# Moving three per-batch transposes to TensorE, regrouping the adapter slots 2, 2, 1, 1, and splitting the last pair's values by score tile

## The chip, the cores and the metric

The kernel runs on one core of one Trainium2 chip. The metric is the device time of one launch in microseconds (us). Five runs of the kernel before gave 178.95, 179.54, 181.83, 183.27 and 183.28 us; their median is 181.83 us. The engines are called PE (TensorE), DVE (VectorE), ACT (ScalarE), POOL (GpSimd) and SP (SyncE, which here only issues transfers).

## The reference, cut to what matters

Four batches of eight heads, 768 positions, head size 64. Attention is masked by a hash: a query sees only the keys whose six sign bits agree with its own. The attention output, laid out as 3072 rows of 512, goes through a mixture of eight rank-16 adapters, two for each row.

```
q_bits = (q @ proj > 0);  k_bits = (k @ proj > 0)          # six bits each
scores = where(q_bucket == k_bucket, q @ k.T / 8, -1e9)
attn   = softmax(scores);  attn_out = attn @ v
x      = attn_out, transposed to (B*S, H*D)                # 3072 x 512
logits = x @ w_gate                                        # eight per row
two largest logits per row -> weights w
out    = x + sum over the two experts of w * (x @ A[e]) @ B[e]
```

## The kernel before, in words

The unit of work is a pair of heads: 16 pairs, four in each batch (`PPB` is 4). For a pair the score matrix is 2 heads x 6 key blocks x 768 queries, which is nine score tiles of 128 x 1024 in PSUM. `score(p, s)` (lines 306 to 315) issues two or three matmuls for tile s and one ACT exponential that writes it to SBUF in bf16. The hash is carried in the contraction: rows 64 to 69 of the operand tile `aug` are sign rows, so one matmul of 71 rows gives score and mask together. There are two score buffers (`ps_s`), so the matmuls of a tile wait until the exponential two tiles earlier is done.

The order of everything is written out by hand. `run` (line 554) walks over pairs p and over steps s = 0 to 8; each step issues a score tile and then some work for other pairs, chosen in `pair(p, s)` (line 599) and `moe_slot(p, s)` (line 532). Each engine takes its instructions in that order.

- `trans` (228) turns queries and keys by PE (`tr`) and copies them out of PSUM (`qkT`, line 244 on DVE, or 242 on ACT when `on_act`). Group 2 for pair p + 1 is at s = 0; groups 0 and 1 for pair p + 2 are at s = 4 and 5. Group 0 goes to ACT in pairs that have adapter work (`has_moe`, 528).
- `cast` (271, s = 1) puts them into `aug` on POOL. `hash` (251, s = 2) forms the signs (`hs` on PE, `sgn` on DVE, line 260) and issues two of the four sign transfers; `hash_b` (266, s = 5) issues the other two, for the pair's second head.
- `uniform` (s = 3) makes a constant (`un`, `uni`) that `norm` adds in line 365, except in the last four pairs, where PE adds it by a matmul (line 331).
- `pvmm` (319) multiplies attention by values: head 0 of pair p at s = 6, 7, 8, and head 1 of pair p - 1 at s = 1 and 3. Its accumulator `pv` is the single buffer of `ps_v`, so head 1 starts (line 320, s = 1) only after `norm(p - 1, 0)` at s = 0 has read it: lines 365 (add), 368 (reciprocal), 370 (product into `x`). `norm(p - 1, 1)` is at s = 4 and is followed by the bf16 copy `xb` on POOL (376).
- `xturn` (412, s = 5) turns `xb` of pair p - 1 into `xT` by a DMA transpose on SP. `xtrans` (420) does the same by PE, with up to six 128 x 128 transposes into a `ps_t` tile and a copy out by DVE (430); before, only the last pair and the one ahead of it use it.
- The adapters of a batch start in the second pair of the next batch (p = 5, 9, 13). A row slot is 128 rows; a batch has six. `lgz` (434, line 445, four matmuls of `lz` for each slot) needs `xT` of all four pairs of the batch. Then come `route_a`, `route_e`, `route_b` (454 to 490: `top`, `d`, `e` on ACT, `gw`, `zm`, `ss`, `rt`), `zmtrans` (498, 504), and `delta` (512 on PE; 519 on DVE adds to `x`), and a transfer out. Slots go in groups of two over three pairs for the first two batches, and in groups of three over two pairs for the third.

`ps_t` has two buffers and holds `tr`, `hs`, `un`, `xtp` (the PE-turned `xb`), in the last pair also one `pvl` and an `lz`. `ps_m` has one buffer, for `lz`, `ztp` and `dl`.

The last pair (`last_pair`, 634) orders its score tiles by thirds of the query blocks: tiles 0 to 2 belong to third 0, 3 to 5 to third 1, 6 to 8 to third 2. `third(u, part)` (380, line 398) multiplies a third by values in two parts; the second part ends with a reciprocal and a product on DVE (402, 408). After it come the adapters of the fourth batch, two slots for each third. Four of the six final additions are on POOL (517), each from a product that ACT makes (516).

Of the kernel before, what the change touches and what calls it, by code (L numbers as in the profile page):

```python
# [19 lines left out]
class Emitter:  # L20
# [355 lines left out]
            nc.gpsimd.tensor_copy(out=self.xb[b][:, hp], in_=self.x[b][:, :, hp * P:(hp + 1) * P])  # L376

    def third(self, u, part):  # L380
        nc, P, T, D = self.nc, self.P, self.T, self.D
        p, b = self.n_pairs - 1, self.B - 1
        if part == 0:
            pool, tag = (self.ps_t, "t") if u == 1 else (self.ps_v, "v")
            pv = pool.tile([P, 2, 2, D + 1], F32, tag=tag, name=f"pvl{u}")
            ri = self.smallp.tile([P, 2, 2], F32, tag="ri", name=f"ril{u}")
            self.pvl[u] = pv, ri
            nc.tensor.matmul(
                out=pv, lhsT=self.eps, start=True, stop=False,
                rhs=self.vb[p % 3][:, :, T, :].unsqueeze(2).to_broadcast([P, 2, 2, D + 1]))  # L390
        pv, ri = self.pvl[u]
        for h in range(2):
            kts = range(T) if h == 0 else range(2) if part == 0 else range(2, T)
            if h == 0 and part:
                continue
            for e in range(2):
                for kt in kts:
                    nc.tensor.matmul(out=pv[:, h, e, :], lhsT=self.p_at(p, h, kt, 3 * e + u),  # L398
                                     rhs=self.vb[p % 3][:, h, self.slot(kt), :], start=False,
                                     stop=(part == 1 and e == 1 and kt == T - 1))  # L400
        if part:
            nc.vector.reciprocal(out=ri, in_=pv[:, :, :, D])
            self.third_x(u, self.xb[b][:, self.PPB - 1])

# [120 lines left out]
            nc.sync.dma_start(out=rows[:, slots[0]:slots[0] + len(slots), :], in_=acc[:, 0:len(slots), :])  # L525


    def has_moe(self, p):
        b, g = divmod(p - self.PPB - 1, self.PPB)
        return 0 <= b < self.B - 1 and g < (3 if b < self.B - 2 else 2)  # L530

    def moe_slot(self, p, s):
        b, g = divmod(p - self.PPB - 1, self.PPB)
        if b < 0 or b > self.B - 2:
            return
        n = 2 if b < self.B - 2 else 3
        if n * g >= self.T:
            return
        slots = tuple(range(n * g, n * g + n))
        if s == 0:  # L540
            self.lgz(b, slots, (0,))
        if s == 1:
            self.lgz(b, slots, tuple(range(1, n)))
            self.route_a(b, slots, now=False)
        if s == 2:
            self.route_e(b, slots)
        if s == 3:
            self.route_b(b, slots)
        if s == 4:
            self.zmtrans(b, slots)  # L550
        if 0 <= s - 6 < n:
            self.delta(b, slots, s - 6)
# [46 lines left out]
    def pair(self, p, s):  # L599
        if s == 0:  # L600
            self.norm(p - 1, 0)
            self.trans(p + 1, 2)
            self.load_qk(p + 3, (0,))
        if s == 1:
            self.pvmm(p - 1, 1, 0, 3)
            self.cast(p + 1, 0)
            self.cast(p + 1, 1)
        if s == 2:
            self.hash(p + 1)
            self.load_qk(p + 3, (1,))  # L610
        if s == 3:
            self.uniform(p)
            self.pvmm(p - 1, 1, 3, 6)
        if s == 4:
            self.norm(p - 1, 1)
            self.trans(p + 2, 0, on_act=self.has_moe(p))
        if s == 5:
            self.xturn(p - 1)
            self.hash_b(p + 1)
            self.vcast(p + 1)  # L620
            self.trans(p + 2, 1)
            if p < 4:
                self.load_moe(p + 1)
            if p == 3:
                self.load_moe(5)
        if s == 6:
            self.pvmm(p, 0, 0, 2)
        if s == 7:
            self.pvmm(p, 0, 2, 4)
        if s == 8:  # L630
            self.pvmm(p, 0, 4, 6)
            self.load_v(p + 3)

    def last_pair(self, p, b):
        t = [(0, 1), (2, 3), (4, 5)]
        x = self.x[b][:, :, (self.PPB - 1) * self.P:]
        for s in range(9):
            self.score(p, s)
            if s == 0:
                self.norm(p - 1, 0)  # L640
                self.pvmm(p - 1, 1, 0, 3)
            if s == 1:
                self.pvmm(p - 1, 1, 3, 6)
                self.norm(p - 1, 1)
            if s == 3:
                self.third(0, 0)
            if s == 4:
                self.third(0, 1)
            if s == 5:
                self.xtrans(p - 1)  # L650
                self.xtrans(p, t[0])
                self.third_x(0, x)
            if s == 6:
                self.third(1, 0)
                self.lgz(b, t[0])
                self.route_a(b, t[0], now=False)
            if s == 7:
                self.route_e(b, t[0])
                self.third(1, 1)
                self.route_b(b, t[0])  # L660
            if s == 8:
                self.xtrans(p, t[1])
                self.zmtrans(b, t[0])
                self.third(2, 0)
                self.third_x(1, x)
        self.third(2, 1)
        self.lgz(b, t[1], far=True)
        self.route_a(b, t[1])
        self.delta(b, t[0], 0, last=True, by_pool=True)
        self.xtrans(p, t[2])  # L670
        self.route_b(b, t[1])
        self.delta(b, t[0], 1, last=True, by_pool=True)
        self.lgz(b, t[2])
        self.zmtrans(b, t[1], last=True, far=True)
        self.route_a(b, t[2])
        self.delta(b, t[1], 0, last=True, by_pool=True)
        self.third_x(2, x)
        self.route_b(b, t[2])
        self.zmtrans(b, t[2], last=True, far=True)
        self.delta(b, t[1], 1, last=True, by_pool=True)  # L680
        for i in range(2):
            self.delta(b, t[2], i, last=True)
# [47 lines left out]
```

## Time and profile before

| what | value |
|---|---|
| median of five runs | 181.83 us |
| the profiled execution's own time | 178.92 us |
| its span | 177.1 us |
| PE, ACT, POOL, DVE busy | 92%, 86%, 65%, 63% of the span |
| granted TensorE clock | 0.99 of full speed |
| 144 exponentials (line 315) | 140.3 us, 1030 ns each |
| 14 DMA transposes (line 416) | 1251 ns of SP each, in the median |

The profile is one execution, with times from the start of its span. The span is cut in 40 slices whose digits are busy tenths; PE shows 9 in nearly every slice from the second to the 37th. A matmul's record includes its way through the array, so matmuls overlap in the records: eighteen value matmuls are issued in 0.55 us, while their records cover 0.72 us. In the chain of waits the first of these figures is what counts.

### The profile page before, as it was taken

What the parts mean: (1) busy time and instruction counts of PE and PEld (TensorE: products, weight loads), DVE (VectorE), ACT (ScalarE), POOL (GpSimd) and SP (SyncE); (2) the same over time, 40 slices, a digit from 0 to 9 for tenths busy, and PEclk for the clock granted to TensorE, in tenths of its full rate; (3) what the DMA queues carried; (4) which work ended last, traced back from release to release, by engine and by line L of the source; (5) the groups of instructions that cost most, each with busy time, mean ns of one, the idle gap of its engine ahead of it and who ended that gap; (6) DMA issues with size and microseconds to landing.
All of it is one profiled execution on the core that took longest, in us unless ns stands there. A gap on an engine that the chain in (4) does not pass through costs nothing.

```text
span 177.1 us, 5185 instructions
## 1 busy us (share of the span) xinstructions
PE 162.1 (92%) x2073; PEld 111.8 (63%) x2074; DVE 111.7 (63%) x294; ACT 151.6 (86%) x174; POOL 115.5 (65%) x140
## 2 busy tenths in 40 slices
PE   7989999999996999999999999999999999989630
PEld 6356585857675666767577676667576774767500
DVE  4663574747474586869674786868554967536860
ACT  3678999999997998999999999999998998988440
POOL 8299998787976477565676476765677546710190
PEclk9999999999999999999999999999999999999995
DMA  5936599798998577697886488977884033540045
GB/s 163 329 135 184 160 262 102 214 122 223 108 251 105 177 125 239 188 152 261 146 257 147 142 133 295 129 208 228 170 262 122 4 97 137 52 183 4 0 157 198
DMA packets 32406, 29.10 MB, mean 164 GB/s; under 512 B 17430, under 2 KB 30590, under 8 KB 32382
## 3 DMA queue, kind: packets, MB, share of 16 engines
q1 hardware_dynamic: 27420, 28.50, 63.3%
q0 software_dynamic: 4832, 0.27, 4.7%
q8 instruction: 16, 0.26, 0.7%
q14 instruction: 8, 0.07, 0.1%
q10 hardware_dynamic: 130, 0.00, 0.0%
HBM read 19.42 MB, written 6.29 MB: 145 GB/s over the span
## 4 chain that ended last, share of the span: by engine, by line
PE 80%; DVE 5%; DMA 4%; ACT 3%; issue 2%; POOL 2%; POOLq 1%; SPq 0%
PE s L313 34%; PE pv L320 17%; PE tr L237 10%; PE hs L257 7%; ACT P L315 3%; PE lz L445 3%; PE dl L512 3%; DMA xT<-xb 2%; POOL acc L517 1%; DMA aug<-sgn 1%; PE warm L184 1%; PE pvl L398 1%; PE trf L125 1%; PE hsd L139 1%; POOLq L725 1%
## 5 line engine op out<-in xcount | busy, mean ns | idle before, releaser
L315 ACT ACTIVATE P<-s 128x1024 bf16<-128x1024 f32 x144 | 140.3, 1030 | 12.4 <-PE s L313 11.4
L313 PE MATMUL s<-aug 71*128 71x256 bf16 (+1 forms) x396 | 86.3, 320 | 2.9 <-issue 1.3
L275 POOL CAST aug<-qkT 64x1536 bf16<-64x1536 f32 x30 | 43.9, 1463 | 15.1 <-DVE qkT L244 14.2
L320 PEld LDWEIGHTS <-P 128*128 128x128 bf16 x1080 | 42.1, 97 | 11.5 <-DVE x L370 3.5
L313 PEld LDWEIGHTS <-aug 71*128 71x128 bf16 x396 | 33.1, 97 | 22.9 <-issue 11.6
L320 PE MATMUL pv<-vb,P 128*128 128x65 bf16 x1080 | 45.2, 193 | 0.2 <-DVE x L370 0.2
L376 POOL CAST xb<-x 128x768 bf16<-128x768 f32 x15 | 12.4, 824 | 26.2 <-DVE x L370 22.0
L237 PE MATMUL tr<-ident,nat 128*128 128x128 f32 x180 | 27.2, 272 | 0.0
L244 DVE TENSOR_SCALAR qkT<-tr 128x512 f32<-128x512 f32 x38 | 25.4, 683 | 2.7 <-PE tr L237 1.4
L237 PEld LDWEIGHTS tr<-ident,nat 128*128 128x128 f32 x180 | 21.8, 140 | 4.8 <-issue 0.6
L365 DVE TENSOR_TENSOR pv<-pv,uni 128x390 f32<-128x390 f32 x24 | 13.6, 567 | 10.9 <-PE pv L320 10.5
L519 DVE SCALAR_TENSOR_TENSOR acc<-dl,rt,x 128x512 f32<-128x512 f32 x20 | 14.9, 748 | 7.9 <-PE dl L512 7.9
L260 DVE TENSOR_SCALAR sgn<-hs 128x384 bf16<-128x384 f32 x15 | 8.4, 558 | 16.9 <-PE hs L257 16.9
L370 DVE TENSOR_TENSOR x<-pv,ri 128x384 f32<-128x384 f32 x30 | 16.7, 557 | 1.0
L221 POOL TENSOR_TENSOR vs<-vn 128x384 f32<-128x384 f32 x16 | 15.9, 994 | 0.0
L219 POOL CAST vb<-vn 128x768 bf16<-128x768 f32 x16 | 13.2, 827 | 0.1
L257 PE MATMUL hs<-qkT,proj 128*32 128x384 f32 x120 | 12.8, 498 | 0.0
L517 POOL TENSOR_TENSOR acc<-tmp,x 128x512 f32<-128x512 f32 x4 | 4.9, 1271 | 9.2 <-ACT tmp L516 9.2
L445 PE MATMUL lz<-wa,xT 128*128 128x136 bf16 x96 | 9.2, 223 | 1.2 <-DMA xT<-xb 1.2
L512 PE MATMUL dl<-Bcat,zmT 128*128 128x512 bf16 x23 | 8.8, 382 | 1.2 <-ACT zmT L502 0.7
L368 DVE RECIPROCAL ri<-pv 128x6 f32<-128x6 f32 x30 | 5.8, 193 | 3.9 <-PE pv L320 3.1
L224 POOL TENSOR_TENSOR vb<-vs,vs 128x128 bf16<-128x128 f32 x16 | 7.3, 459 | 1.3
(65 smaller groups left out, 111.8 us busy)
## 6 DMA issues: line engine op xcount, KB each, us to landing
vn<-in_v_dram SPq DMA_DIRECT2D x16, 384.0 KB
nat<-in_q_dram SPq DMA_DIRECT2D x15, 384.0 KB
nat<-in_k_dram SPq DMA_DIRECT2D x15, 384.0 KB
out_dram<-acc SPq DMA_DIRECT2D x6, 512.0 KB
out_dram<-acc SPq DMA_DIRECT2D x2, 768.0 KB
out_dram<-acc SPq DMA_DIRECT2D x6, 256.0 KB
aug<-sgn SPq DMA_DIRECT2D x60, 9.0 KB
nat<-in_q_dram SPq DMA_DIRECT2D x2, 192.0 KB
```

Source lines behind the costliest of these rows:

```text
L221: nc.gpsimd.tensor_add(out=s3, in0=vn[:, :, 0:3, :], in1=vn[:, :, 3:6, :])
L237: nc.tensor.transpose(out=ps[:, j * P:(j + 1) * P], in_=self.nat[p][:, idx % 2, idx // 2, u * P:(u + 1) * P], identity=self.ident)
L244: nc.vector.tensor_scalar(out=out, in0=ps, scalar1=2.0 ** -5, scalar2=None, op0=ALU.mult)
L257: nc.tensor.matmul(out=ps[32 * j:32 * j + 32, :], lhsT=self.proj2, rhs=self.qkT[p][:, j * 384:(j + 1) * 384], start=True, stop=True)
L275: self.nc.gpsimd.tensor_copy(out=self.aug[p % 2][0:64, :, e * n:(e + 1) * n], in_=self.qkT[p][64 * e:64 * e + 64, :].rearrange("p (j c) -> ...
L313: nc.tensor.matmul(out=ps[:, o:o + n], lhsT=aug[0:71, 2 * h + 1, kt * P:(kt + 1) * P], rhs=q, start=True, stop=True)
L315: nc.scalar.activation(out=self.P_[p][:, s * 1024:(s + 1) * 1024], in_=ps, func=ACT.Exp, scale=128.0)
L320: self.nc.tensor.matmul(out=pv, lhsT=self.p_at(p, h, kt, i), rhs=self.vb[p % 3][:, h, self.slot(kt), :], start=(start and kt == 0), stop=( ...
L370: nc.vector.tensor_tensor(out=self.x[b][:, :, c:c + D].rearrange("p (u e) d -> p e u d", e=2), in0=pv[:, 0:T, 0:D].rearrange("p (e u) d -> ...
L445: nc.tensor.matmul(out=lz[:, i, :], lhsT=self.xT[b][:, t, s * P:(s + 1) * P], rhs=self.wa[:, t, :], start=(t == 0), stop=(t == self.nD - 1))
L512: nc.tensor.matmul(out=ps, lhsT=self.zmT[b, slots][:, i * P:(i + 1) * P], rhs=self.Bcat, start=True, stop=True)
L519: nc.vector.scalar_tensor_tensor(out=acc[:, i, :], in0=ps, scalar=self.rt[b, slots][:, i:i + 1], in1=self.x[b][:, slots[i], :], op0=ALU.mu ...
```

## The change

Five edits, all in the written-out order:

1. At the first pair of the next batch (p = 4, 8, 12) the DMA transpose of a batch's last pair is dropped, and at the end of s = 8 `xtrans(p - 1)` turns it by PE, with the copy on DVE.
2. For the first two batches the groups of slots become (0, 1), (2, 3), (4), (5) over all four pairs. The third batch keeps 3 and 3. In a pair with a group of one slot, group 0 of `trans` is copied out by DVE, not by ACT.
3. For the last pair, the two sign transfers of its second head are issued in s = 2 of pair 14, not in s = 5 behind that pair's DMA transpose.
4. `third` has three parts, each of the four key blocks that one score tile holds; in steps 2 to 4, 5 to 7, and 8 and after.
5. In the last pair `xtrans(14)` goes from s = 5 to s = 4; behind the last score tile the order changes, and the first `zmtrans` goes behind the last third, its copy on ACT (line 502) in place of DVE.

```diff
@@ third(u, part)
-        for h in range(2):
-            kts = range(T) if h == 0 else range(2) if part == 0 else range(2, T)
-            if h == 0 and part:
-                continue
+        for j in range(4):
+            h, kt = divmod(4 * part + j, T)
             for e in range(2):
-                for kt in kts:
-                    nc.tensor.matmul(out=pv[:, h, e, :], lhsT=self.p_at(p, h, kt, 3 * e + u),
...
-        if part:
+        if part == 2:
@@ moe_group(p), in place of has_moe; moe_slot takes its slots from it
+        groups = ((0, 1), (2, 3), (4,), (5,)) if b < self.B - 2 else ((0, 1, 2), (3, 4, 5), (), ())
+        return b, groups[g]
@@ pair(p, s)
         if s == 2:
             self.hash(p + 1)
+            if p + 1 == self.n_pairs - 1:
+                self.hash_b(p + 1)
...
-            self.trans(p + 2, 0, on_act=self.has_moe(p))
+            self.trans(p + 2, 0, on_act=len(self.moe_group(p)[1]) > 1)
         if s == 5:
-            self.xturn(p - 1)
-            self.hash_b(p + 1)
+            if p % self.PPB:
+                self.xturn(p - 1)
+            if p + 1 < self.n_pairs - 1:
+                self.hash_b(p + 1)
...
         if s == 8:
             self.pvmm(p, 0, 4, 6)
+            if p % self.PPB == 0:
+                self.xtrans(p - 1)
@@ last_pair(p, b)
-            if s == 3:
-                self.third(0, 0)
+            if 2 <= s < 5:
+                self.third(0, s - 2)
             if s == 4:
-                self.third(0, 1)
+                self.xtrans(p - 1)
             if s == 5:
-                self.xtrans(p - 1)
                 self.xtrans(p, t[0])
                 self.third_x(0, x)
+            if 5 <= s < 8:
+                self.third(1, s - 5)
             if s == 6:
-                self.third(1, 0)
                 self.lgz(b, t[0])
                 self.route_a(b, t[0], now=False)
             if s == 7:
                 self.route_e(b, t[0])
-                self.third(1, 1)
                 self.route_b(b, t[0])
             if s == 8:
                 self.xtrans(p, t[1])
-                self.zmtrans(b, t[0])
+                self.third_x(1, x)
                 self.third(2, 0)
-                self.third_x(1, x)
         self.third(2, 1)
         self.lgz(b, t[1], far=True)
         self.route_a(b, t[1])
+        self.third(2, 2)
+        self.zmtrans(b, t[0], last=True)
+        self.xtrans(p, t[2])
         self.delta(b, t[0], 0, last=True, by_pool=True)
-        self.xtrans(p, t[2])
         self.route_b(b, t[1])
+        self.lgz(b, t[2])
         self.delta(b, t[0], 1, last=True, by_pool=True)
-        self.lgz(b, t[2])
         self.zmtrans(b, t[1], last=True, far=True)
```

More of the change, by code (lines that the diff above doesn't have):

```diff
@@ L391, in third @@
         pv, ri = self.pvl[u]
-        for h in range(2):
-            kts = range(T) if h == 0 else range(2) if part == 0 else range(2, T)
-            if h == 0 and part:
-                continue
+        for j in range(4):
+            h, kt = divmod(4 * part + j, T)
             for e in range(2):
-                for kt in kts:
-                    nc.tensor.matmul(out=pv[:, h, e, :], lhsT=self.p_at(p, h, kt, 3 * e + u),
-                                     rhs=self.vb[p % 3][:, h, self.slot(kt), :], start=False,
-                                     stop=(part == 1 and e == 1 and kt == T - 1))
-        if part:
+                nc.tensor.matmul(out=pv[:, h, e, :], lhsT=self.p_at(p, h, kt, 3 * e + u),
+                                 rhs=self.vb[p % 3][:, h, self.slot(kt), :], start=False,
+                                 stop=(part == 2 and j == 3 and e == 1))
+        if part == 2:
             nc.vector.reciprocal(out=ri, in_=pv[:, :, :, D])
@@ L525, in delta, with moe_group @@
             nc.sync.dma_start(out=rows[:, slots[0]:slots[0] + len(slots), :], in_=acc[:, 0:len(slots), :])
-    def has_moe(self, p):
+    def moe_group(self, p):
         b, g = divmod(p - self.PPB - 1, self.PPB)
-        return 0 <= b < self.B - 1 and g < (3 if b < self.B - 2 else 2)
+        if not 0 <= b < self.B - 1:
+            return b, ()
+        groups = ((0, 1), (2, 3), (4,), (5,)) if b < self.B - 2 else ((0, 1, 2), (3, 4, 5), (), ())
+        return b, groups[g]
     def moe_slot(self, p, s):
-        b, g = divmod(p - self.PPB - 1, self.PPB)
-        if b < 0 or b > self.B - 2:
+        b, slots = self.moe_group(p)
+        n = len(slots)
+        if not n:
             return
[L536 to L539, printed above, removed]
         if s == 0:
```

## The prediction

> **What bounds the kernel now.** I read the page's chain shares first, then busy time in single pairs, then the chain and the timelines around each edit.
>
> ```profile
> PE 80%; DVE 5%; DMA 4%; ACT 3%; issue 2%; POOL 2%; POOLq 1%; SPq 0%
> ```
>
> PE carries the chain. How hard it binds is seen by cutting single pairs out: no adapters (28.42 and 124.74), two slots (66.37 and 114.89), columns PE, PE weights, DVE, ACT, POOL.
>
> ```profile
> 28.42:37.34 8.92, 8.76 (x120) 6.15 (x118) 5.30 (x12) 8.57 (x10) 7.25 (x9) 1.00 0.92 166
> 66.37:76.21 9.84, 9.74 (x131) 6.82 (x130) 7.55 (x22) 9.37 (x12) 6.39 (x8) 1.00 0.85 198
> 114.89:124.74 9.85, 9.75 (x131) 6.83 (x130) 7.56 (x22) 9.38 (x12) 6.41 (x8) 1.00 0.79 199
> 124.74:133.70 8.96, 8.80 (x119) 6.08 (x118) 5.10 (x11) 8.63 (x10) 6.56 (x8) 1.00 0.75 224
> ```
>
> A pair lasts 8.92 to 8.96 us without adapters, 9.85 with two slots. PE is full in both, ACT half a microsecond behind. So PE work added to a pair counts unless a PE wait absorbs it.
>
> Two places are neither. The chain shows them:
>
> ```profile
> 51.64 0.83 POOL xb L376
> 52.49 4.42 DMA xT<-xb
> 57.63 0.55 PE pv L320 x18
> ...
> 153.52 2.31 DMA aug<-sgn
> 155.83 0.05 issue
> 155.88 0.41 PE s L313 x2
> 156.28 0.02 issue
> 156.31 1.03 ACT P L315
> ```
>
> Pair 5's first `lz` waits for the transpose issued at 52.49; the wait list has 1.4 us there for PE's weights, and ACT then idles 1.37. Pair 9 loses only about 0.1 (its four `lz` take 0.36 in the chain, those of pair 10 take 0.24), pair 13 nothing. Tile 1 of the last pair waits for signs issued at 153.5; ACT idles 0.75.
>
> **What the Trainium skill says.** "DMA: Bandwidth & Descriptors", section Anatomy of one DMA, puts most of a transfer's fixed cost, about 2 us, into the receipt at the end. The trace agrees for the signs (2.31 us); the transpose took 4.42. "PSUM — Partial Sum Buffer", section Engine vs sequencer instructions: the vector and scalar queues are strict FIFO and matmuls complete in program order. The trace agrees: DVE's `norm` stands behind whatever precedes it. "TensorE: Matmul & The Clock Gate", section PE-mode transpose: the result lands in PSUM and needs a DVE copy, about 275 ns in a kernel. Here a record is 221 ns, but six follow each other in 0.35 us of chain, so I use 0.33 of issue.
>
> **The change, part by part.**
>
> *PE transposes in pairs 4, 8, 12.* Each adds six transposes (0.33 us of PE) and one 128x768 copy (0.56 us, line 430) and removes one DMA transpose from SP (1.25 us; the sign transfers behind it go earlier, which nothing waits for there). In pair 4 PE stands still 0.16 us before pair 5's tile 0 and takes 0.59 for it instead of 0.44: 0.31 us of waiting for ACT covers the 0.33. Without that cover it would be 0.33 each time.
>
> The copy costs more than the transposes: DVE does it ahead of `norm(p - 1, 0)`, which frees the only `pv` buffer, and queued behind the waiting value matmuls on PE are tile 2, the hash and tile 3. In pair 9 now, value matmuls end issue at 94.16 and drain at 94.32; `norm` runs 94.36 to 95.75 and the next values start at 96.30. After: transposes 94.16 to 94.49, drained 0.2 later, copy 94.70 to 95.26, `norm` (starts 0.60, 0.23 apart, then 0.56) 95.30 to 96.70, values 96.76: +0.46. In pair 13 `norm` has no add (0.20 + 0.56): 134.76 against the present 134.65, +0.1. In pair 5 the same sum gives 54.25 + 2.60 = 56.86 against 57.46 now: the DMA wait goes but a wait for `norm` takes its place, −0.6 and not −1.3. `xT` itself is ready at 55.4, ahead of `lz` at 55.5.
> Sum: −0.6 + 0.46 + 0.1 = **0.0**.
>
> *Groups 2, 2, 1, 1 (pairs 7, 8, 11, 12).* PE work is the same over the batch: one slot is four `lz` at 0.059 = 0.24, `ztp` 0.055, `dl` 0.21: 0.5 us. ACT loses one `qkT` copy (0.59 record, 0.5 between neighbours), DVE gains one (0.60 from start to start). That one stands ahead of the `zmT` copy, for which `dl` waits, and behind `dl` stand the value matmuls and tile 7. Pair 11 on DVE now:
>
> ```profile
> 118.08 0.56 DVE L260 TENSOR_SCALAR sgn<-hs 128x384 bf16<-128x384 f32 x1 [0.79 <-PE hs L257]
> 118.65 0.29 DVE L352 COPY uni<-un 128x130 f32<-128x130 f32 x1
> 118.86 0.35 DVE L476 SCALAR_TENSOR_TENSOR gw<-lz,top,e 128x8 f32<-128x8 f32 x2
> 119.24 0.42 DVE L478 TENSOR_TENSOR zm<-lz,gw 128x256 bf16<-128x256 f32 x1
> ...
> 120.68 0.56 DVE L370 TENSOR_TENSOR x<-pv,ri 128x384 f32<-128x384 f32 x1
> 121.15 0.28 DVE L504 COPY zmT<-ztp 128x256 bf16<-128x256 bf16 x1
> ```
>
> DVE is in one piece from 118.08, and `dl` starts at 121.49, just as PE gets to it. With one slot, one `gw` (0.17) and half of `zm` (0.13) go, so the chain is 0.30 earlier; then `qkT` puts 0.60 in: `zmT` starts 121.45, ends 121.66, `dl` 121.72. PE gets there at 121.41: a new stall of 0.3 us. A pair with two slots that gets one: −0.5 + 0.3 = −0.2. A pair with none that gets one: +0.5 + 0.3 = +0.8, less about 0.2 that PE spends waiting for ACT at tiles 7 and 8 (0.50 and 0.55 in the chain where two matmul groups take 0.43) = +0.6. Together +0.4 a batch, two batches: **+0.8**. Bounds: −0.3 a batch, if the stall is covered and ACT's relief counts, to +0.8, if nothing is absorbed.
>
> *Signs in pair 14.* The two transfers (1.5 us of SP) come before any load, since there is none left; they can land near 153, tile 1 needs them at 155.4. ACT goes on at 155.5: **−0.75**.
>
> *Thirds, and the end.* Here most of the 0.75 is lost again. A third's last part still follows its last tile. The PSUM buffer of third 1 is the one `xtrans(14)` used: its copy ends about 1.3 us after third 0 and third 1 is now asked for 0.9 after, so PE waits 0.4 and ACT idles about 0.35 at tile 6; before, the same wait came one step later and cost 0.59 at tile 7. Tile 8's exponential ends near 163.8 instead of 164.62. Then `lz` of slots 2 and 3, whose PSUM buffer comes free with line 408's `x`, is moved ahead of the last part: now 165.56 to 165.58, after about 164.56. The last part queues behind it (0.47), and `top`, `d` (0.45 of DVE) stand ahead of its reciprocal: last `xb` 165.9 against 166.0. First `dl` stands behind the transposes of that `xb`, so ACT's first product is at 166.9 against 166.94. That starts what ends the kernel:
>
> ```profile
> 167.69 4.94 POOL L517 TENSOR_TENSOR acc<-tmp,x 128x512 f32<-128x512 f32 x4 [9.16 <-ACT tmp L516]
> ```
>
> Four additions back to back, then transfers. They start about 0.1 earlier. So edits 3 to 5 together give **−0.1**, between −0.75 (all kept) and +0.3 (new order later than the old).
>
> *Sum:* 0.0 + 0.8 − 0.1 = **+0.7 us** on the profiled execution's 178.92 (span 177.1 and 1.8 around it): 179.6. That execution is in the lower of two groups of runs (178.95, 179.54; 181.83 to 183.28). The mean of five is 181.37, the median 181.83. A median of five jumps between the groups, so I put the change on the mean: **182.1 us**.
>
> **The rivals.**
>
> A. *Both waits gone, little put in their place.* If PE's lead hides the `norm` wait and the 0.3 stalls: −1.2 (pair 5), −0.1, −0.75 kept, groups 0: −2.0, or 179.4. For it: ACT loses 1.0 us of copies over two batches and DVE is only 76% busy in adapter pairs. Against: pairs without a DMA wait already show a wait for line 370 of up to 0.6, ten times.
>
> B. *DVE becomes the bound, slower.* Place: `zmT` ahead of `dl` in pairs 7, 8, 11, 12. If the DVE queue is late there by 1.2 us and not 0.3, because ACT's late `e` holds `gw` too, each costs 0.9 more: 0.7 + 3.6 = +4.3, or 185.7. It decides from a stall of about 1.0 on (+3.5). Against: DVE has 2.3 us free in such a pair.
>
> C. *The upper runs are late transposes.* If in those runs pairs 9 and 13 also wait 1.3 for the DMA, taking it away puts them near the lower group: 181.4 − 2 × 1.3 = 178.8 to 179.6. For it: one landing took 4.42 us, others left no wait. Against: 0.1 seen in pair 9, and no trace of an upper run.
>
> **How the numbers follow.** My forecast 0.5, A 0.25, C 0.15, B 0.06, the rest for what I do not see. The forecast's own range is 179.6 to 184: the two groups plus 0.7. A and C lie at 178.8 to 179.6, so the low end is 178.2 (lowest run less 0.75, the signs alone); the high end 184.2 is the highest run plus 0.9. B is left out. About 2% is what a measurement of this kernel can tell from no change: 178.2 and 185.5. My forecast lies inside, A and C at their faster ends (0.08), B beyond the other end (0.06): same 0.86.
>
> **What would show it.** Right: no `xT` wait in pair 5, but 0.5 to 0.7 us of PE waiting for line 370 there and in pair 9; PE waiting near 0.3 for `zmT` in four pairs; pairs 7 and 8 at about 9.65 and 9.55; no sign wait at the last pair; POOL's four additions starting as long before the span's end as now (9.4 us). Wrong: pairs 8 and 12 under 9.2, or values of pair 9 no later after tile 0 than now, or a last stage shorter by over 0.5.

## The result, and the profile after

The ratio of the changed kernel to the kernel before is 1.0038 (95% interval 1.0022 to 1.0054): a slow-down of 0.4%, about 0.7 us, clear of the spread and far within 2%. The medians over all runs, 179.82 us (44 runs) and 179.96 us (79 runs), show it the other way round because 22 of the 79 runs of the kernel before lie above 181.21 us, the slowest of the changed kernel's, and the ratio leaves out runs as far up as these. The profiled execution took 179.35 us (before: 178.92), its span 177.6 us (177.1).

The page's chain shares after. PE's share has fallen from 80% to 68%, DVE's has risen from 5% to 13%; DMA, 4% before, is gone.

```profile
PE 68%; DVE 13%; POOL 7%; ACT 4%; issue 3%; POOLq 1%
```

The transfers that the chain held are out of it, and vector work has come in. To see where, both kernels are cut into pairs, from the first `tr` record of one pair to that of the next. Kernel before, pairs 5, 7, 8, 9, 11, 12 and 13 (columns: length, then busy time of PE, PE weights, DVE, ACT, POOL, then granted clock, DMA share, GB/s):

```profile
55.01:66.20 11.19, 9.92 (x131) 6.82 (x130) 7.45 (x22) 9.48 (x12) 6.24 (x8) 1.00 0.56 129
76.05:85.90 9.85, 9.75 (x132) 6.83 (x131) 7.56 (x22) 9.38 (x12) 6.41 (x8) 1.00 0.78 199
85.90:94.91 9.01, 8.85 (x120) 6.15 (x118) 5.40 (x12) 8.66 (x10) 6.55 (x8) 1.00 0.78 222
94.91:104.88 9.97, 9.87 (x132) 6.83 (x130) 7.46 (x22) 9.38 (x12) 6.25 (x8) 1.00 0.66 139
114.73:124.58 9.85, 9.75 (x132) 6.83 (x131) 7.56 (x22) 9.38 (x12) 6.41 (x8) 1.00 0.79 198
124.58:133.53 8.95, 8.79 (x119) 6.08 (x118) 5.06 (x12) 8.62 (x10) 6.55 (x8) 1.00 0.75 224
133.53:143.93 10.40, 10.36 (x139) 7.37 (x137) 6.45 (x20) 9.55 (x12) 6.67 (x8) 1.00 0.26 64
```

The changed kernel, the same pairs:

```profile
54.82:65.25 10.43, 9.92 (x131) 6.75 (x130) 8.24 (x23) 9.47 (x12) 6.22 (x8) 1.00 0.59 123
75.10:84.81 9.71, 8.99 (x125) 6.42 (x124) 6.97 (x20) 8.96 (x11) 6.76 (x8) 1.00 0.95 201
84.81:94.55 9.74, 9.16 (x130) 6.68 (x130) 6.58 (x20) 8.99 (x11) 6.41 (x8) 1.00 0.62 189
94.55:104.98 10.43, 9.92 (x132) 6.75 (x131) 8.25 (x23) 9.35 (x12) 5.99 (x8) 1.00 0.57 130
114.83:124.59 9.76, 8.99 (x125) 6.42 (x125) 7.00 (x20) 9.01 (x11) 6.80 (x8) 1.00 0.89 200
124.59:134.19 9.60, 9.28 (x130) 6.73 (x130) 6.26 (x18) 8.90 (x11) 6.39 (x7) 1.00 0.60 190
134.19:144.58 10.39, 10.35 (x138) 7.29 (x137) 7.10 (x22) 9.51 (x12) 6.39 (x7) 1.00 0.28 62
```

Pair 5 is 0.76 us shorter, pair 9 0.46 longer and now exactly as long as pair 5: both wait for the same thing. Pairs 8 and 12, which got a slot, grew by 0.73 and 0.65; pairs 7 and 11, which gave one away, shrank by 0.14 and 0.09 only. In these two PE's busy time fell from 9.75 to 8.99 while the length hardly moved. But the trace has records of only 19 of the 24 `dl`, and those of the four pairs with one slot are missing; one `dl` fills 0.22 us. So PE stands still for about 0.5 us there, before for 0.1.

Why pairs 5 and 9 are alike shows in the changed kernel's timeline of pair 9 (DVE, and the value matmuls of head 1 on PE):

```profile
94.32 0.56 DVE L426 COPY xT<-xtp 128x768 bf16<-128x768 bf16 x1 [1.53 <-PE xtp L424]
94.79 0.56 DVE L365 TENSOR_TENSOR pv<-pv,uni 128x390 f32<-128x390 f32 x1
95.39 0.20 DVE L368 RECIPROCAL ri<-pv 128x6 f32<-128x6 f32 x1
95.62 0.56 DVE L370 TENSOR_TENSOR x<-pv,ri 128x384 f32<-128x384 f32 x1
...
96.23 0.72 PE L320 MATMUL pv<-vb,P 128*128 128x65 bf16 x18 [0.41 <-DVE x L370]
```

DVE sits idle for 1.53 us, then does the copy just when `norm` could start; PE pays 0.41 us, its weight load 0.9. Pair 11 shows the other wait, first the weight load of `dl` in the kernel before, then the stretch in the changed kernel:

```profile
121.48 0.10 PEld L512 LDWEIGHTS <-zmT 128*128 128x128 bf16 x1 [0.31 <-DVE zmT L504]
```

```profile
120.73 0.68 DVE L244 TENSOR_SCALAR qkT<-tr 128x512 f32<-128x512 f32 x1
...
121.33 0.21 DVE L500 COPY zmT<-ztp 128x128 bf16<-128x128 bf16 x1
...
121.60 0.10 PEld L508 LDWEIGHTS <-zmT 128*128 128x128 bf16 x1 [0.62 <-DVE zmT L500]
121.83 0.53 PE L320 MATMUL pv<-vb,P 128*128 128x65 bf16 x12 [0.57 <-DVE zmT L500]
```

The `zmT` copy stands behind a `qkT` copy that ACT did before; `dl` waits for it, and the value matmuls behind `dl`. The weight load's idle time has grown from 0.31 to 0.62 us. The 0.57 us ahead of the value matmuls is not all stall, since the `dl` without a record ran in it for 0.22. How long PE itself waits is seen in the trace of run 1 (the groups alone), which has the record, in the same pair:

```profile
123.96 0.39 PE L512 MATMUL dl<-Bcat,zmT 128*128 128x512 bf16 x1 [0.34 <-DVE zmT L504]
```

In the kernel before PE waits 0.04 us there. At the end the first POOL addition starts 23.49 us after pair 14 begins (168.07 less 144.58); before it was 23.76 (167.69 less 143.93). So the stage of the last edits is 0.27 us shorter.

### The profile page after: what moved, and what is told of

It is laid out like the page before. It is cut to its first block, busy times and chain, and to the rows that moved or that the text cites. A ratio compares the mean times of both kernels' runs of the same rounds, so it can differ in the third digit from the quotient of the medians.

```text
span 177.6 us, 5224 instructions
## 1 busy us (share of the span) xinstructions
PE 161.0 (91%) x2087; PEld 112.3 (63%) x2092; DVE 114.7 (65%) x308; ACT 151.8 (85%) x175; POOL 115.2 (65%) x140
## 4 chain that ended last, share of the span: by engine, by line
PE 68%; DVE 13%; POOL 7%; ACT 4%; issue 3%; POOLq 1%
PE s L313 28%; PE pv L320 15%; PE tr L237 8%; PE hs L257 7%; ACT P L315 4%; PE lz L441 3%; DVE pv L365 2%; PE dl L508 2%; DVE x L370 2%; POOL acc L513 2%; POOL xb L376 2%; POOL vs L221 2%; POOL vb L219 1%; DVE sgn L260 1%; PE warm L184 1%
## 5 line engine op out<-in xcount | busy, mean ns | idle before, releaser
L313 PEld LDWEIGHTS <-aug 71*128 71x128 bf16 x396 | 32.6, 97 | 21.3 <-issue 10.5
L244 DVE TENSOR_SCALAR qkT<-tr 128x512 f32<-128x512 f32 x40 | 27.0, 683 | 2.3 <-POOL aug L275 1.3
L508 PE MATMUL dl<-Bcat,zmT 128*128 128x512 bf16 x19 | 7.2, 382 | 1.4 <-ACT zmT L498 1.0
L223 POOL TENSOR_TENSOR vs<-vs 128x128 f32<-128x128 f32 x16 | 7.3, 454 | 1.3
```

The costliest lines, as they stand in the source:

```text
L244: nc.vector.tensor_scalar(out=out, in0=ps, scalar1=2.0 ** -5, scalar2=None, op0=ALU.mult)
L313: nc.tensor.matmul(out=ps[:, o:o + n], lhsT=aug[0:71, 2 * h + 1, kt * P:(kt + 1) * P], rhs=q, start=True, stop=True)
```

## The experiments

Each kernel was timed on one chip beside the kernel before, and profiled. Because the start, up to pair 5, varies by 2.4 us from execution to execution in the profiles (54.55 to 56.94 us), single stages are compared as lengths inside a trace.

**1. Groups alone.** The kernel before with edit 2:

```diff
...
+        groups = ((0, 1), (2, 3), (4,), (5,)) if b < self.B - 2 else ((0, 1, 2), (3, 4, 5), (), ())
...
-            self.trans(p + 2, 0, on_act=self.has_moe(p))
+            self.trans(p + 2, 0, on_act=len(self.moe_group(p)[1]) > 1)
```

> Kernel before with the groups 2, 2, 1, 1 alone (and DVE in place of ACT for the copy in pairs with one slot). Theory (the pair with a new slot pays its PE work and a new stall ahead of dl, because the zmT copy stands behind a qkT copy on DVE): pairs 7 and 11 shorter by 0.1 each, pairs 8 and 12 longer by 0.65 to 0.75 each, so +1.1 to +1.3 us, ratio near 1.0065. Rival (pairs 8 and 12 grew because of the six PE transposes there, 0.33 us each on a full PE): +0.4 to +0.6 us, ratio near 1.003.

Measured: ratio 1.0218 (1.0144 to 1.0292), median 184.51 us; a miss for both. Of the slots' own cost the trace shows what the theory says (pairs 7 and 8 together 9.71 + 9.72 = 19.43 us, before 18.86; pairs 11 and 12 19.29, before 18.80). Most of the rest is three waits for the DMA transpose, in pairs 5, 9 and 13 (1.44, 1.17 and 0.79 us of PE), where before there was one, of 1.17:

```profile
L445 PE MATMUL lz<-wa,xT 128*128 128x136 bf16 x96 | 9.5, 223 | 3.4 <-DMA xT<-xb 3.4
```

In pair 8 the transpose is issued at 93.41 and `lz` goes on at 98.10, 4.7 us later; before it was 92.39 and at most 95.7, 3.3 us. The wait for the signs at the last pair is longer too, 0.97 us of PE and not 0.50. So with DMA transposes kept, regrouping costs some 4 us; edit 1 keeps that from happening. The two edits are not a sum.

**2. Turns alone.** The kernel before with edit 1:

```diff
-            self.xturn(p - 1)
+            if p % self.PPB:
+                self.xturn(p - 1)
...
             self.pvmm(p, 0, 4, 6)
+            if p % self.PPB == 0:
+                self.xtrans(p - 1)
```

> Kernel before with the PE transposes in pairs 4, 8 and 12 alone. Theory: pair 5 gives back 0.75, pair 9 pays 0.46 for the vector copy ahead of norm, pair 13 nothing, the transposes themselves are covered: -0.3 us, ratio near 0.998. Rival (the transposes are what lengthens pairs 8 and 12): about +0.4 us, ratio 1.002. In the trace: PE waits for line 370 by 0.4 or more in pairs 5 and 9, and pair 8 as long as before (8.96).

Measured: ratio 1.0015 (0.9986 to 1.0043). By this alone the rival's 1.002 would stand and the theory's 0.998 just fail. The trace decides by stages: pair 8 is 9.03 us long, as before (9.01): the six transposes cost nothing there, against the rival. Pair 9 is 10.43, as in the changed kernel. From pair 5 to pair 14 it takes 88.64 us against 88.92: −0.28, as the theory has it. The profiled execution, at 181.38 us, loses more than that later: it waits 1.57 us for the signs of the last pair, the kernel before in its profile 0.50. Whether such waits hide the 0.28 in the other executions too is not shown. From here to the changed kernel's 89.76 between pairs 5 and 14 the groups add 1.12 us, the theory's 1.1 to 1.3.

**3. Last pair alone.** The kernel before with edits 3 to 5 of the diff above.

> Kernel before with the edits around the last pair alone: early signs, thirds in three parts, new order at the end. Theory: the exponential of the last tile ends 0.7 earlier, the first POOL addition only 0.3 earlier, because the new order of the end gives 0.4 back: -0.3 us, ratio near 0.9985. Rival (the early signs are worth their whole wait): -0.75 us, ratio 0.996.

Measured: ratio 1.0016 (0.9989 to 1.0043), against both. In the trace the last exponential starts 18.97 us after pair 14 begins (before 19.67) and the first POOL addition 23.47 us (before 23.76): 0.70 and 0.29 earlier, as the theory has it. To the end of the span it is 32.96 us (before 33.17). The profiled execution, at 181.10 us, lost its time in pair 5, which is told in the last section. Why the ratio shows no gain over all runs stays open. What the edits are made of is told apart better by the next run and by run 7.

**4. Signs alone.** The kernel before with edit 3:

```diff
             self.hash(p + 1)
+            if p + 1 == self.n_pairs - 1:
+                self.hash_b(p + 1)
...
-            self.hash_b(p + 1)
+            if p + 1 < self.n_pairs - 1:
+                self.hash_b(p + 1)
```

> Kernel before with only the two sign transfers of the last pair issued in step 2 of pair 14. Theory (the wait at tile 1 goes, but the later wait for a PSUM buffer at third 1 and the zm wait at the end stay): -0.5 to -0.75 us, since the old end keeps what it is given; ratio 0.996 to 0.997. Rival (what is gained at tile 1 is lost again at the next wait, the PSUM buffer of third 1): -0.1 or less, ratio 0.999 or more.

Measured: ratio 0.9944 (0.9908 to 0.998). The theory holds, and the rival's 0.999 lies outside the interval. Its last exponential and its first POOL addition:

```profile
162.26 1.01 ACT L315 ACTIVATE P<-s 128x1024 bf16<-128x1024 f32 x1
...
166.34 4.93 POOL L517 TENSOR_TENSOR acc<-tmp,x 128x512 f32<-128x512 f32 x4 [9.15 <-ACT tmp L516]
```

From pair 14's start (143.27) to that exponential 18.99 us, before 19.67: 0.68 of the 0.75 us that ACT idled for the signs are kept. From there to POOL 4.08, before 4.09.

**5. Copy on ACT.** The changed kernel with ACT doing the `qkT` copy in pairs with one slot too:

```diff
-            self.trans(p + 2, 0, on_act=len(self.moe_group(p)[1]) > 1)
+            self.trans(p + 2, 0, on_act=len(self.moe_group(p)[1]) > 0)
```

> The changed kernel, with the qkT copy of group 0 on ACT also in pairs with one slot. Theory (PE is full there, and the DVE queue ahead of zmT makes the stall ahead of dl): the stalls of 0.25 to 0.5 in pairs 7, 8, 11 and 12 go, the changed kernel gets shorter by 0.6 to 1.0 us, so ratio to the kernel before 0.998 to 1.001. Rival (ACT is as full as PE, its 0.5 us of copy shows): no gain, or up to 1 us longer, ratio 1.004 to 1.009.

Measured: ratio 1.0007 (0.9982 to 1.0031). Waits for DVE's `zmT` fall from 3.5 us in eight places to 1.2 in four, on the weight load, and vanish on the value matmuls (1.7 in three places before, 0.22 of each being a `dl` without a record). The ratio lies in the theory's range, and the rival's 1.004 lies outside the interval. Pairs 5 to 14 take 89.37 us against 89.76: 0.39 won, less than the 0.6 to 1.0 that the theory named. So the stall is real and is made by the order on DVE, but the copy isn't free on ACT either, which is then busy for 9.35 of the 9.62 us of pair 7.

**6. Turn at step 7.** The changed kernel with `xtrans(p - 1)` one step earlier:

```diff
             self.pvmm(p, 0, 2, 4)
+            if p % self.PPB == 0:
+                self.xtrans(p - 1)
         if s == 8:
             self.pvmm(p, 0, 4, 6)
-            if p % self.PPB == 0:
-                self.xtrans(p - 1)
```

> The changed kernel with the PE transposes at step 7, not 8, so that the vector copy runs before norm has anything to do. Theory: pair 5 gives 0.5 more and pair 9 loses nothing, -0.9 to -1.0 us against the changed kernel; ratio to the kernel before near 0.998. Rival (0.33 us of PE in step 7 has no wait to cover it): -0.3 us or less, ratio 1.002 or more.

Measured: ratio 0.9972 (0.9949 to 0.9995). Pair 9 in this kernel's timeline:

```profile
93.52 0.56 DVE L426 COPY xT<-xtp 128x768 bf16<-128x768 bf16 x1 [0.73 <-PE xtp L424]
...
94.33 0.57 DVE L365 TENSOR_TENSOR pv<-pv,uni 128x390 f32<-128x390 f32 x1 [0.24 <-PE pv L320]
...
95.78 0.72 PE L320 MATMUL pv<-vb,P 128*128 128x65 bf16 x18
```

The same copy, 0.8 us earlier, is done before `norm` asks for DVE, and the values start 0.45 us earlier than at 96.23. Pair 9's first part, up to its next turned queries, is 4.82 us as in the kernel before, not 5.28; pair 5's is 4.81. Pairs 5 to 14 take 88.80 us against 89.76. The theory holds.

**7. Old end.** The changed kernel with the old order behind the last tile:

```diff
                 self.xtrans(p, t[1])
+                self.zmtrans(b, t[0])
+                self.third(2, 0)
                 self.third_x(1, x)
-                self.third(2, 0)
         self.third(2, 1)
+        self.third(2, 2)
         self.lgz(b, t[1], far=True)
         self.route_a(b, t[1])
-        self.third(2, 2)
-        self.zmtrans(b, t[0], last=True)
...
```

> The changed kernel with the old order behind the last score tile (thirds still in three parts, the last part ahead of lz of slots 2 and 3, the first zmT copy on DVE). Theory: from the end of the last exponential to the first POOL addition 3.1 us as in the kernel before, not 3.5: -0.4 us against the changed kernel, ratio near 1.0015. Rival (the wait for zm comes back and costs as much): no difference, ratio 1.004.

Measured: ratio 1.0024 (0.9999 to 1.0049). The last exponential and the first POOL addition, first in the changed kernel, then here:

```profile
163.56 1.02 ACT L315 ACTIVATE P<-s 128x1024 bf16<-128x1024 f32 x1
...
168.07 4.93 POOL L513 TENSOR_TENSOR acc<-tmp,x 128x512 f32<-128x512 f32 x4 [9.56 <-ACT tmp L512]
```

```profile
164.91 1.02 ACT L315 ACTIVATE P<-s 128x1024 bf16<-128x1024 f32 x1
...
168.99 4.93 POOL L513 TENSOR_TENSOR acc<-tmp,x 128x512 f32<-128x512 f32 x4 [9.14 <-ACT tmp L512]
```

4.51 us in the new order, 4.08 in the old. The theory's 0.4 is there in the trace; the ratio's interval holds the theory's 1.0015 and the rival's 1.004, so it can't show it alone. And with thirds in three parts the stretch from pair 14 to that exponential is 18.98 us, with two parts (run 4) 18.99: in that stretch splitting the thirds is worth nothing, and run 10 asks the same of the whole.

**8. Put together.** The changed kernel with the transposes at step 7 (run 6), the old end (run 7) and groups of 2, 2, 2, of which only the last is shown:

```diff
...
-        groups = ((0, 1), (2, 3), (4,), (5,)) if b < self.B - 2 else ((0, 1, 2), (3, 4, 5), (), ())
+        groups = ((0, 1), (2, 3), (4, 5), ()) if b < self.B - 2 else ((0, 1, 2), (3, 4, 5), (), ())
...
```

> Early signs, thirds in three parts, the old order at the end, PE transposes at step 7, groups 2, 2, 2 as before. Theory: pair 5 -1.25, pair 9 -0.1, last pair -0.7, nothing paid: -2.0 us, ratio 0.989. Rival (gains do not add, a wait taken away shows the next): -0.7 us or less, ratio 0.996 or more.

Measured: ratio 0.9898 (0.9851 to 0.9944), median 177.41 us. The theory's 0.989 lies in the interval, the rival's 0.996 outside it: the gains add.

**9. Late transfer.** Groups alone, with the transfer out of slot 5 issued in step 3 of the next pair.

```diff
...
-        elif i == len(slots) - 1:
+        elif i == len(slots) - 1 and slots != (5,):
...
+        if s == 3 and slots == (0, 1) and b or s == 3 and slots == (0, 1, 2):
+            rows = self.out[(b - 1) * self.S:b * self.S, :].rearrange("(p t) f -> p t f", t=self.T)
+            self.nc.sync.dma_start(out=rows[:, 5:6, :], in_=self.acc[b - 1, (5,)][:, 0:1, :])
...
```

> The groups 2, 2, 1, 1 alone, as in the run groups alone, but the transfer out of the slot done in pairs 8 and 12 is issued in step 3 of the pair behind it, so that nothing follows the DMA transpose closely on its queue. Theory (that transfer, 256 KB, is what makes the transpose land at 4.4 to 4.7 us and not at 3.2): the waits for xT in pairs 9 and 13 fall to 0.3 or less each, 1.5 to 2 us shorter than groups alone, ratio near 1.01. Rival (the landing does not depend on it): waits of 0.8 to 1.4 stay in pairs 9 and 13, ratio near 1.02.

Measured: ratio 1.015 (1.0065 to 1.0236), an interval that holds both. The waits decide. They stay, 1.24 us of PE in pair 9 and 1.01 in pair 13: the theory falls, the transfer behind the transpose is not what makes it land late. In the 2 us up to 99.00, in which most of the wait of pair 9 lies, the DMA engines hardly work (last two columns: their share, GB/s):

```profile
97.00:99.00 2.00, 1.07 (x10) 0.79 (x8) 1.68 (x4) 1.54 (x2) 0.51 (x2) 1.00 0.06 8
```

So it isn't other traffic at that moment either; in the 2 us before, the share is 0.71, and what that traffic does to the transpose was not tried. Why a transpose lands after 3.3 us in one pair and after 4.7 in another stays open.

**10. Turn at 7 and signs.** The kernel before with edit 1 at step 7 and edit 3, nothing else.

> The kernel before with two edits: PE transposes at step 7 of pairs 4, 8, 12, and the early signs. Thirds, order of the end and groups as before. Theory (thirds in three parts are worth nothing, within 0.15 us): same as the version put together, ratio near 0.99. Rival (levelling the thirds is worth part of the gain): 0.3 us or more slower than it, ratio 0.992 or more.

Measured: ratio 0.9858 (0.9805 to 0.9911), median 176.9 us. From pair 14 to the end it takes 32.69 us, the version put together 32.68. The rival's 0.992 or more lies outside the interval. The theory holds by the traces; to show 0.15 us the interval is too wide. This is the version to keep: two small moves, 1.4% faster than the kernel before (0.9% at the interval's upper end), and so faster than the changed one.

## Why the prediction was right and wrong

The step that failed is the base of the sum, "I put the change on the mean". The mean of the five runs, 181.37 us, stands 0.46 us under their median, 181.83, with which the time is compared. So 182.1 us stands only 0.27 us, 0.15%, over it, though the sum of the parts, +0.7 us on 178.92, is +0.39%. Measured is +0.38% (0.22 to 0.54). Put on that median, as 182.5, the sum would have named the change that was found.

The same step took for granted that the changed kernel keeps both groups of runs, "the two groups plus 0.7". The runs showed otherwise: its 44 runs lie between 179.0 and 181.21 us, and none reaches 182.1. The range held (the median, 179.82, lies in 178.2 to 184.2).

| term | predicted, us | measured in the traces, us |
|---|---|---|
| pair 5 (DMA wait out, `norm` wait in) | −0.6 | −0.76 |
| pair 9 (copy ahead of `norm`) | +0.46 | +0.46 |
| pair 13 | +0.1 | −0.01 |
| pairs 7 and 11 | −0.2 each | −0.14, −0.09 |
| pairs 8 and 12 | +0.6 each | +0.73, +0.65 |
| last pair and end | −0.1 | −0.27 |
| sum | +0.66 | +0.57 |

That the sum comes so near is in part luck. The groups cost 1.15 us and not 0.8; pair 5, pair 13 and the end came out 0.16, 0.11 and 0.17 us better than forecast, which makes up for it.

- Transposes by PE: covered, as forecast (pair 8 with them alone 9.03 us, before 9.01). The copy ahead of `norm` was the price; run 6 took it away by moving it and got it back. Shown.
- Groups: the extra stall ahead of `dl` is there and has the size forecast, 0.3 us (the weight load's idle time from 0.31 to 0.62, PE's wait from 0.04 to 0.34). Run 5 shows the DVE order to be its cause. The working left out a term on both sides, and that the stall still came out right is luck: in step 1 the slot's four `lz` (0.24 us) go too, so that in pair 11 PE gets to the last turned queries ahead of `dl` 5.39 us after the pair's start and not 5.69, and DVE to `sgn` after 3.11 and not 3.35. What was too small is the sum of a batch, +0.59 and +0.56 and not +0.4. The terms (−0.2 and +0.8) give +0.6 if nothing is taken off for PE's waiting for ACT, so the 0.2 taken off was too much; and the bound "if nothing is absorbed" is that +0.6 and not +0.8. What was also not seen is that edit 2 leans on edit 1: alone it costs 2.2%.
- Signs: the wait goes, and up to the last exponential 0.68 us of the forecast 0.75 are kept (run 4: 0.68, the changed kernel: 0.69).
- Thirds and end: forecast as eaten up, and it is, but at one place only. The wait for the PSUM buffer of third 1 costs ACT 0.33 us, as forecast (0.35); the new order of the end costs 0.42 (run 7). The net is −0.27.
- Rival A had no stalls behind the waits: false, both are in the trace. Rival B, DVE late by 1.2 us: false, 0.3. Rival C asked whether a late transpose in pairs 9 and 13 makes the upper runs. The count of runs speaks for a wider form of it, with the signs' wait beside the transpose's: of the six kernels with edits 1 and 3 (the changed one, runs 5 to 8 and 10) none of 122 runs lies above 181.21 us; of the three with one of the two (runs 2 to 4) 9 of 60 do, and of the kernel before 22 of 79. In the traces both waits differ from kernel to kernel, that of pair 5 from 0.67 to 1.53 us and that of the signs from 0.50 to 1.57, and runs 1 and 9 wait 0.8 to 1.2 us in pairs 9 and 13. But there is no trace of an upper run of the kernel before, so the cause of these runs is not shown.

## What to carry to other kernels

A copy that takes the place of a transfer must be put where its engine is idle, not where its input happens to be free: one step earlier, the same copy cost pair 9 nothing. In an order written by hand, evening out the work of one engine moves copies onto another, and what counts is what each copy then stands in front of. And a predicted change belongs on the very number that it will be compared with.

## What the runs showed of the hardware

A transpose by DMA from SBUF to SBUF had landed 3.3 us after its issue in one pair (pair 8 of the kernel before) and took 4.4 to 4.8 us in others. In run 9 this was not because of the transfer behind it, and the DMA engines were at 0.06 of their time in a stretch of that wait.

In the profile of the last pair's edits alone, TensorE's granted clock fell after a wait of 1.53 us for that transpose (the column behind POOL's is the clock):

```profile
56.00:58.00 2.00, 0.47 (x6) 0.23 (x4) 0.90 (x2) 0.74 (x1) 1.04 (x1) 1.00 0.21 43
58.00:60.00 2.00, 2.00 (x27) 1.68 (x25) 0.21 (x2) 1.02 (x1) 1.88 (x2) 0.61 0.85 260
60.00:62.00 2.00, 2.00 (x11) 0.25 (x10) 0.21 (x2) 1.24 (x2) 0.00 (x0) 0.53 0.42 141
62.00:64.00 2.00, 2.00 (x35) 1.65 (x32) 1.83 (x8) 1.38 (x2) 0.00 (x0) 1.00 0.00 0
```

The hash of that pair took 1.49 us and not 0.85, and the pair's first part, up to its next turned queries, 7.98 us and not 6.05, 1.9 us more. In pair 5 of the kernel before PE waited too, for 1.17 us, and in run 1 for 1.44 us, with no such fall. So of the 1.9 us some 0.4 are the longer wait, and the rest goes with the lower clock. This is one trace; that the wait made the clock fall is not shown.
